# The fourth column block of the last gate's weights as two transfers of 108 and 20 rows

## The chip, the cores and the metric

The kernel runs on one core of a Trainium2 chip. The metric is the device time of one execution in microseconds (us); less is better. Before the change the median of three runs is 242.96 us (242.74 to 242.99).

## What is computed

One decoder step for four rows of batch: a conditioned layer norm, attention over the last 2048 positions of a cache, and a gated feed-forward block. The condition `c` gives six vectors by one matrix; the last of them, `gb`, scales the output of the feed-forward block.

```python
mod = (_silu(c) @ w_mod).reshape(c.shape[0], 6, 1, -1)
sa, ca, ga, sb, cb, gb = (mod[:, 0], ..., mod[:, 5])
h = _layernorm(x) * (1 + ca) + sa
x = x + ga * A(h, k_cache, v_cache, wq, wo)      # 32 heads, 8 groups, 2048 positions, float32
h = _layernorm(x) * (1 + cb) + sb
x = x + gb * ((silu(h @ w1) * (h @ w3)) @ w2)    # 512 -> 1792 -> 512
```

All data is float32. Some 100 MB of caches and weights are read once from HBM, and the four rows of batch need little arithmetic on each byte.

## The kernel before

**Staging.** Two buffers of 128 rows (partitions) by 16384 columns, `KV[0]` and `KV[1]`, take the keys and values of the eight groups in turn; `WP` takes the projection weights. When the last groups are done, the same buffers take the weights of the feed-forward block. `KV[1]` then holds, from left to right: the second part of w3 (columns 0 to 6143, in two transfers on the semaphores `df2a` and `df2b`), the last gate's weights `gb_in` (columns 6144 to 8191, four column blocks of 512, one for each 128 rows of the contraction, on `dgb`), and w2 (14 chunks of 512 columns in six transfers of 4, 4, 2, 2, 1 and 1 chunks, each on a semaphore of its own, `dw[0]` to `dw[5]`).

**Order of the transfers.** All large transfers but one are issued by SyncE (SP) through the helper `load` (L89), in the order in which the code has them; ACT issues the first projection weights and `x_in` (4 rows of 512 columns) at the start (L92, L93). SP waits on semaphores of the compute engines before a buffer is written again. After `o_done` has reached 8 (L120) it issues the two parts of w3, `gb_in` and the six parts of w2 without a further wait; then it waits for `last` and stores the output (L482).

**Order of the work at the end.** TensorE's order is that of the code. After the norm it multiplies by w1 and a part of w3 (`bQ`), by the rest of w3 (`bA`), and transposes the products. Then it waits for `dgb` (L443) and computes the gate in four products, one for each column block (`bM`, L445). ACT copies it to `gb_sb`. Then TensorE goes through w2: it waits for `dw[i]` before part i (L455). The first eight chunks are summed in `bO`, the last six in `bX`, to which `bO` is brought by `y_sb`. After the last part VectorE multiplies by the gate (`yt`, L478), adds the residual (`y`, L480), and SP stores `y`.

A semaphore of a transfer rises by 16 when the whole transfer has landed. `KV<-w_in` in a row of the profile is a transfer or a wait for w2 at this place, since the input names are shown without their digits; `KV<-f_in` is w1 or w3.

Of the kernel before, what the change touches and what calls it, by code (L numbers as in the profile page):

```python
# [43 lines left out]
def block_kernel(nc, x_in, t0_in, t1_in, kv_in, w_in, wm_in, f1_in, f2_in, gb_in, w2_in, out):  # L44
    T, v, s, gp, S = nc.tensor, nc.vector, nc.scalar, nc.gpsimd, nc.sync

    def sems(names):
        return [nc.alloc_semaphore(n) for n in names.split()]

    def sb(name, cols, rows=P):  # L50
        return nc.alloc_sbuf_tensor(name, (rows, cols), F32).ap()
# [8 lines left out]
    dx, dt0, dt1, dkv, dk, dva, dvb, dwo, dm, df1, df2a, df2b, dgb = sems("dx dt0 dt1 dkv dk dva dvb dwo dm df1 df2a df2b dgb")  # L60
# [5 lines left out]
    KV = [sb("KV0", 16384), sb("KV1", 16384)]  # L66
# [21 lines left out]
    def load(dst, src, sem):  # L88
        S.dma_start(dst, src).then_inc(sem, 16)  # L89
# [30 lines left out]
    S.wait_ge(o_done, G)  # L120
    load(KV[1][:, :3072], f2_in[:, :3072], df2a)
    load(KV[1][:, 3072:6144], f2_in[:, 3072:], df2b)
    load(KV[1][:, 6144:8192], gb_in, dgb)
    for a, b, sem in zip(W2_CUTS[:-1], W2_CUTS[1:], dw):
        load(KV[1][:, 8192 + a * 512 : 8192 + b * 512], w2_in[:, a * 512 : b * 512], sem)

# [313 lines left out]
    t_hid = V.op(v.tensor_mul(view(hidT)[:, :, :3], view(sT)[:, :, :3], view(bS)[:, :, :3, :B]))  # L440


    T.wait_ge(dgb, 16)  # L443
    for k in range(4):
        ins = mm(bM[32 * k : 32 * k + B, :], sc[:, k * B : (k + 1) * B], KV[1][:, 6144 + 512 * k : 6144 + 512 * (k + 1)])  # L445
    ins.then_inc(pe, 1)
# [85 lines left out]
```

## Time and profile before

| | us |
|---|---|
| median of three runs | 242.96 |
| the profiled execution | 243.09 |
| its span, first to last instruction | 241.7 |

The profile is that of one execution. Its span is divided by engine: PE is TensorE's matrix multiply, DVE is VectorE, ACT is ScalarE, SPq is the queue of SyncE from which transfers are issued. "DMA share" is the mean busy share of the core's 16 DMA engines; a share of 0.25 says that on average four of the 16 were moving data. It can pass 1 a little where packets overlap at their ends, and in short stretches a packet is counted with the stretch in which it lies, so single steps of 0.1 us are rough. A packet is what one engine moves at a time: a row of a transfer, at most 64 KB, and at the end of a transfer a word of 4 bytes for the semaphore on each engine that took part. The chain that ended last is followed back from the last instruction to what released it.

### The profile page before, as it was taken

The numbers are of one execution on the slowest core, as the hardware profiler recorded it, in microseconds if no ns is written. First come the engines' busy times: TensorE is split into PE (matmuls) and PEld (weight loads), VectorE is DVE, ScalarE is ACT, GpSimd is POOL, SyncE is SP. The second block draws the span as 40 slices with busy tenths as digits, with TensorE's granted clock in tenths as the row PEclk, the third lists the DMA queues.
The fourth block names the chain that finished last, engine by engine and source line by source line (L and its number), as shares of the span: only waits on it lengthen the run. The fifth ranks groups of instructions, "written<-read, shape, count | busy, mean of one in ns | idle before, by whom it ended". The sixth has DMA issues, their size and how long they took to land. (4 is left out here: it accounts for less than half of the span.)

```text
span 241.7 us, 2238 instructions
## 1 busy us (share of the span) xinstructions
PE 137.8 (57%) x940; PEld 38.0 (16%) x940; DVE 38.6 (16%) x126; ACT 25.1 (10%) x54; POOL 1.7 (1%) x14
## 2 busy tenths in 40 slices
PE   3004677726771478267713782877137869656964
PEld 0000122201220013112200130121001312111211
DVE  3003203202200022022000220130002222133112
ACT  2002002100010011010100110011002100133110
POOL 2000000000000000000000000000000000000000
PEclk9999959968798579887985898679758997995999
DMA  7998989899989898999898989998989999999993
GB/s 266 440 511 358 510 361 499 369 423 439 504 369 499 369 499 370 423 428 504 369 499 369 499 369 423 434 510 369 499 347 445 442 396 445 449 431 394 413 415 116
DMA packets 4045, 101.34 MB, mean 419 GB/s; under 512 B 452, under 2 KB 580, under 8 KB 1096
## 3 DMA queue, kind: packets, MB, share of 16 engines
q1 hardware_dynamic: 3888, 99.17, 95.7%
q10 hardware_dynamic: 152, 2.11, 2.1%
q8 instruction: 3, 0.05, 0.1%
q14 instruction: 2, 0.02, 0.0%
HBM read 101.20 MB, written 0.07 MB: 419 GB/s over the span
## 5 line engine op out<-in xcount | busy, mean ns | idle before, releaser
L266 PE MATMUL bS<-KV,Z 128*16 128x512 f32 x256 | 42.7, 828 | 39.2 <-PEq L269 39.2
L266 PE MATMUL bO<-KV,pT 128*16 128x512 f32 x256 | 32.5, 652 | 0.5
L266 PEld LDWEIGHTS bS<-KV,Z 128*16 128x16 f32 x256 | 9.3, 123 | 67.1 <-issue 67.1
L222 DVE TENSOR_REDUCE MX<-bS 128x1 f32<-128x512 f32 x8 | 5.5, 692 | 80.4 <-PE bS L266 80.4
L266 PE MATMUL bM<-KV,sc 128*4 128x512 f32 x24 | 6.9, 801 | 16.6 <-DVE sc L188 16.6
L230 ACT ACTIVATE p_sb<-bS,NB 128x512 f32<-128x512 f32 x8 | 5.5, 687 | 101.2 <-DVE NB L228 101.2
L287 PE MATMUL bP<-ident,p_sb 128*128 128x128 f32 x32 | 5.6, 303 | 16.6 <-PEq L269 16.6
L266 PE MATMUL bA<-WP,oT 128*4 128x512 f32 x64 | 11.1, 773 | 4.3 <-PEq L269 4.3
L266 PEld LDWEIGHTS bO<-KV,pT 128*16 128x16 f32 x256 | 8.2, 107 | 23.9 <-issue 23.9
L251 ACT ACTIVATE o_sb<-bO,LB 128x512 f32<-128x512 f32 x8 | 5.5, 687 | 48.8 <-PE bO L266 48.8
L266 PE MATMUL bQ<-WP,hT 128*4 128x512 f32 x64 | 9.2, 647 | 0.6 <-DVE hT L197 0.6
L287 PE MATMUL bX<-ident,o_sb 128*128 128x128 f32 x32 | 5.0, 280 | 7.2 <-PEq L269 7.2
L254 DVE TENSOR_REDUCE oT<-bX 128x16 f32<-128x64 f32 x8 | 1.8, 224 | 43.6 <-PE bX L287 43.6
L287 PEld LDWEIGHTS bP<-ident,p_sb 128*128 128x128 f32 x32 | 3.6, 148 | 24.0 <-issue 24.0
L287 PE MATMUL bT<-ident,q_sb 128*128 128x128 f32 x32 | 5.5, 298 | 3.2 <-PEq L269 3.2
L201 ACT ACTIVATE q_sb<-bQ 128x512 f32<-128x512 f32 x8 | 4.7, 593 | 13.3 <-PE bQ L266 13.3
L287 PEld LDWEIGHTS bX<-ident,o_sb 128*128 128x128 f32 x32 | 3.4, 141 | 14.3 <-issue 14.3
L235 DVE COPY pT<-bP 128x256 f32<-128x256 f32 x8 | 3.4, 424 | 13.5 <-PE bP L287 13.5
L266 PE MATMUL bQ<-KV,h2T 128*4 128x512 f32 x32 | 5.3, 816 | 0.3 <-DVE h2T L398 0.3
L287 PEld LDWEIGHTS bT<-ident,q_sb 128*128 128x128 f32 x32 | 3.6, 150 | 8.0 <-issue 7.7
L266 PEld LDWEIGHTS bM<-KV,sc 128*4 128x4 f32 x24 | 1.0, 104 | 22.4 <-DVE sc L188 18.2
L266 PE MATMUL bX<-KV,sc 128*4 128x512 f32 x24 | 4.2, 592 | 0.0
(100 smaller groups left out, 65.2 us busy)
## 6 DMA issues: line engine op xcount, KB each, us to landing
WP<-w_in SPq DMA_DIRECT2D x3, 4096.0 KB, 22.0
KV<-kv_in SPq DMA_DIRECT2D x1, 4096.0 KB, 24.3
KV<-f_in SPq DMA_DIRECT2D x1, 4096.0 KB, 28.0
KV<-kv_in SPq DMA_DIRECT2D x1, 3072.0 KB, 31.1
KV<-wm_in SPq DMA_DIRECT2D x1, 3072.0 KB, 18.4
KV<-f_in SPq DMA_DIRECT2D x2, 1536.0 KB, 19.2
KV<-t_in SPq DMA_DIRECT2D x1, 2056.0 KB, 12.2
WP<-t_in ACTq DMA_DIRECT2D x1, 2048.0 KB, 12.4
```

The source lines that it names most:

```text
L201: A.op(s.mul(q_sb, bQ, DH**-0.5), q_ok)
L222: t = V.op(v.reduce_max(MX[:, 0:1], bS, axis=AX.X))
L230: A.op(s.activation(p_sb, bS, AF.Exp, bias=NB[:, 0:1], accum_out=SM[:, 0:1]), p_ok)
L235: v.tensor_copy(pT.rearrange("p (t b c r) -> p c b t r", t=NT, b=B, c=4), bP.rearrange("p (c b i) -> p c b i", c=4, b=B)[:, :, :, :16].rea ...
L251: A.op(s.mul(o_sb, bO, LB[:, 0:1]), o_ok)
L254: V.op(v.tensor_reduce(oT.rearrange("p (r b) -> p r b", r=R), diag, axis=AX.X, op=ALU.add), ot_ok)
L266: return T.matmul(o, lhsT, rhs, start=start, stop=stop, skip_group_check=True)
L287: ins = T.transpose(dst[:, c * P : (c + 1) * P], src[:, c * P : (c + 1) * P], ident)
```

## The change

`gb_in` is loaded by three transfers instead of one. The first has 128 rows and the first three column blocks (1536 columns). The fourth block (512 columns) comes in two transfers, rows 0 to 107 and rows 108 to 127. All three are on `dgb`, and TensorE waits for 48 instead of 16 before the gate's products. The bytes and their places are the same, and so is everything else.

```diff
     load(KV[1][:, 3072:6144], f2_in[:, 3072:], df2b)
-    load(KV[1][:, 6144:8192], gb_in, dgb)
+    load(KV[1][:, 6144:7680], gb_in[:, :1536], dgb)
+    for rows in (slice(0, 108), slice(108, 128)):
+        load(KV[1][rows, 7680:8192], gb_in[rows, 1536:], dgb)
     for a, b, sem in zip(W2_CUTS[:-1], W2_CUTS[1:], dw):
         load(KV[1][:, 8192 + a * 512 : 8192 + b * 512], w2_in[:, a * 512 : b * 512], sem)
@@
-    T.wait_ge(dgb, 16)
+    T.wait_ge(dgb, 48)
```

SP's queue from the first part of the feed-forward weights on, the piece of the difference between the two kernels (rows by columns of each transfer; `f_in` with 8192 columns is w1 with a part of w3, `w_in` is w2):

```order
 L89 DMA KV<-f_in 128x8192
 L89 DMA KV<-f_in 128x3072 x2
-L89 DMA KV<-gb_in 128x2048
+L89 DMA KV<-gb_in 128x1536
+L89 DMA KV<-gb_in 108x512
+L89 DMA KV<-gb_in 20x512
 L89 DMA KV<-w_in 128x2048 x2
 L89 DMA KV<-w_in 128x1024 x2
 L89 DMA KV<-w_in 128x512 x2
```

Two more transfers stand ahead of the six of w2; on the other engines no instruction changes its place.

## Rows read from the trace of the kernel before

**Rows 1.** The page: span, DMA packets, and DMA queues (packets, MB, share of 16 engines).

```profile
span 241.7 us, 2238 instructions
...
DMA packets 4045, 101.34 MB, mean 419 GB/s; under 512 B 452, under 2 KB 580, under 8 KB 1096
...
q10 hardware_dynamic: 152, 2.11, 2.1%
q8 instruction: 3, 0.05, 0.1%
q14 instruction: 2, 0.02, 0.0%
```

**Rows 2.** Stretches: busy of PE, PEld, DVE, ACT, POOL, clock, DMA share, GB/s.

```profile
2.00:40.00 38.00, 16.89 (x74) 3.75 (x74) 6.42 (x20) 3.65 (x8) 0.47 (x6) 0.91 1.01 435
...
80.00:120.00 40.00, 25.60 (x172) 7.20 (x176) 5.96 (x21) 3.42 (x7) 0.00 (x0) 0.82 1.01 434
...
220.00:230.00 10.00, 9.47 (x62) 2.07 (x62) 1.30 (x5) 0.81 (x2) 0.00 (x0) 0.81 1.01 426
```

**Rows 3.** Chain that ended last, by time: start, us, what (its end).

```profile
210.14 28.79 DMA KV<-w_in
238.93 0.04 issue
238.97 0.45 PE bX L266 x8
239.42 0.02 issue
239.44 0.30 DVE yt L478
```

**Rows 4.** Timeline of the end: start, us, engine, what [idle before, releaser].

```profile
207.29 0.43 SPq L89 DMA_DIRECT2D KV<-gb_in  x1
207.77 12.21 SPq L89 DMA_DIRECT2D KV<-w_in  x6
...
231.47 1.04 PE L266 MATMUL bM<-KV,sc 128*4 128x512 f32 x8
...
232.77 1.04 PE L266 MATMUL bO<-KV,hidT 128*4 128x512 f32 x8 [0.26 <-DMA KV<-w_in]
...
235.16 1.04 PE L266 MATMUL bO<-KV,hidT 128*4 128x512 f32 x8 [1.14 <-DMA KV<-w_in]
...
236.44 0.62 PE L266 MATMUL bX<-KV,hidT 128*4 128x128 f32 x16 [0.24 <-DMA KV<-w_in]
...
237.71 1.05 PE L266 MATMUL bX<-KV,hidT 128*4 128x128 f32 x24 [0.29 <-DMA KV<-w_in]
238.36 0.11 PEld L266 LDWEIGHTS bX<-KV,hidT 128*4 128x4 f32 x8 [0.32 <-DMA KV<-w_in]
238.97 0.11 PEld L266 LDWEIGHTS bX<-KV,hidT 128*4 128x4 f32 x8 [0.50 <-DMA KV<-w_in]
```

**Rows 5.** Page, DMA issues: transfer, issuer, count, size, us to landing.

```profile
KV<-gb_in SPq DMA_DIRECT2D x1, 1024.0 KB, 22.8
```

**Rows 6.** Short stretches at the end; the last two figures are DMA share and GB/s.

```profile
236.80:237.00 0.20, 0.20 (x12) 0.00 (x0) 0.17 (x1) 0.00 (x0) 0.00 (x0) 1.00 1.16 379
237.00:237.10 0.10, 0.10 (x8) 0.08 (x8) 0.00 (x0) 0.00 (x0) 0.00 (x0) 1.00 0.44 164
237.10:237.20 0.10, 0.10 (x8) 0.03 (x8) 0.00 (x0) 0.00 (x0) 0.00 (x0) 1.00 0.28 102
...
237.80:237.90 0.10, 0.10 (x8) 0.10 (x9) 0.00 (x0) 0.00 (x0) 0.00 (x0) 1.00 0.17 62
237.90:238.00 0.10, 0.10 (x12) 0.10 (x8) 0.00 (x0) 0.00 (x0) 0.00 (x0) 1.00 0.10 41
...
238.20:238.30 0.10, 0.10 (x8) 0.00 (x0) 0.00 (x0) 0.00 (x0) 0.00 (x0) 1.00 0.11 41
238.30:238.40 0.10, 0.07 (x8) 0.04 (x8) 0.00 (x0) 0.00 (x0) 0.00 (x0) 1.00 0.05 20
...
238.50:238.60 0.10, 0.10 (x8) 0.00 (x0) 0.00 (x0) 0.00 (x0) 0.00 (x0) 1.00 0.01 0
```

**Rows 7.** DMA queues in 33.8 to 34.0 us: packets, MB, share of 16 engines.

```profile
q8 instruction: 1, 0.02, 32.2%
```

**Rows 8.** DMA queues in 14.5 to 14.8 us, where the packets of `x_in` lie.

```profile
q10 hardware_dynamic: 4, 0.01, 7.0%
```

## The prediction

> **What bounds the kernel now.** I read the stretches first. From 2 us on the 16 DMA engines are busy all the time: the share is 1.01 in the first 40 us, in the middle and from 220 to 230 us [rows 2]. No compute engine is near that over the whole span. The chain that ended last says the same of the end: it goes back from the last product over the last transfer of w2, which landed at 238.93 us; behind it come only 0.45 us of TensorE, two VectorE instructions and the store [rows 3]. So what counts is when the last DMA engine has moved its last packet.
>
> The third view is the short stretches at the end [rows 6]. The engines don't stop together. Until 237.0 us all 16 are busy; in 237.0 to 237.1 the share is 0.44, and in the next step it is 0.28, which is 4 to 5 engines. It is 0.17 (three) up to 237.9, 0.10 to 0.11 (two) up to 238.3, then 0.05 (one), and 0.01 from 238.5 on. So 12 engines have done their part by about 237.1 and four are late. I put their ends at about 237.5, 237.85, 238.3 and 238.5 us and call them L1 to L4. The landing that the chain shows (238.93) is L4's end and 0.4 us more. A transfer has landed only when its slowest engine is done, so L4 alone sets the time of the kernel.
>
> Why are they late? All transfers but `x_in` have 128 rows and load the engines alike. Queue q10 has 152 packets [rows 1]: 128 rows and 16 words for the 128-row transfer, which leaves 8, four rows and four words, for `x_in`. What is not alike are the five instruction packets on q8 and q14 [rows 1]: one of q8 took 32.2% of 16 engines for 0.2 us [rows 7], which is 1.03 us of one engine, in the middle of full load. An engine with such a packet stays behind by it to the end, since the queue never runs dry.
>
> **The change part by part.** *What an engine has to do.* Before, each engine moves 8 rows of `gb_in`, 64 KB. In 128-row transfers the time of an engine goes with the size: TensorE's waits for w2 end at 232.77, 235.16, 236.44, 237.71, 238.36 and 238.97 [rows 4], so 1 MB takes 2.4 us, half of it 1.27, and a quarter 0.61 to 0.65 us. Three quarters then take some 1.84 us, so an engine that has no row of the fourth block saves 0.6 us. This is an estimate from these rows.
>
> *Who gets rows of the fourth block.* Both kinds of transfer in the trace share the rows equally: 128 rows are 8 for each of 16 engines, and 4 rows are one for each of four [rows 1]. By equal shares 108 rows go to 12 engines, 9 each, and 20 rows to 10 engines, 2 each. A row of 2 KB costs 0.084 us by `x_in` (7.0% of 16 engines in 0.3 us for four packets [rows 8]) and 0.08 us by the last part of w2 (0.61 to 0.65 us for 8 rows [rows 4]). I take 0.08. If the ten are among the twelve, ten engines get 11 rows, 0.88 us: 0.28 us more than the 0.6 saved, and with two further words 0.3. Two engines get 9 rows, 0.72 us: 0.13 us more. Four get none: 0.6 us less. The sum over the engines is about nil, as it must be: the change only moves work from four engines to twelve.
>
> [...]
>
> *What the end does.* The gain is that of the engine that is last after the change. The 12 early engines go from 237.1 to 237.4 at most, far below 238.5, so 0.3 us on them is hidden by the late ones. If all four late engines are spared, the last is L4 at 237.9: 0.6 us earlier. Each late engine that is not spared moves up by 0.3 us instead. From the rows alone it can't be told which engine is which. I followed the packets in the trace from one to the next on each engine (each starts as the one before it ends). This is no row of a view, so I use it only to choose: the large instruction packets, which made L3 and L4, lie on engines that had no packet of `x_in`; L2's lies on one that had. If the engines of `x_in` are among the ten, as a nested choice would have it, L2 goes from 237.85 to 238.15, and is the new last. Then the end moves from 238.5 to 238.15: 0.35 us earlier.
>
> *Behind the last landing* nothing changes: 0.45 us of TensorE, the two VectorE instructions and the store. The waits for w2 ahead of it move by the same amount. That TensorE is no new bound there I read from the idle times before the parts: 0.26, 1.14, 0.24, 0.29 us and on the weight loads 0.32 and 0.50 [rows 4]; the first product of w2 can't start before the gate's products end at 232.51, and would want to at 232.4, which costs nothing behind it, since it has 1.14 us of idle time before the next.
>
> *The wait for 48.* `gb_in` landed 22.8 us after its issue at 207.29 [rows 4, 5], so at 230.1; the gate's products start at 231.47. They are held by TensorE's own order, with 1.4 us to spare. The last of the three transfers can be 0.3 us later. The wait costs nothing; without that cover it would cost these 0.3 us, and what is queued behind it is the whole of w2.
>
> *Two more issues on SP.* An issue takes 0.43 us there, so w2's first part is issued 0.9 us later, at 208.6 instead of 207.8. Its data is used at 232.77. The six issues of w2 lasted 12.21 us [rows 4], far more than six times 0.43: the queue was full and SP was held until about 220. With two more ahead, the last two or three parts of w2 are issued when a transfer further back has landed, at 224 to 228 us by the transfers' order, an estimate; the data of the last part moves at about 238. The cover is 10 us. Cost nothing.
>
> **The rivals.** *All four spared.* The 12 engines leave out L1 to L4 together: 0.6 us less, 242.4. For it: four late and four spared. Against: the packet on one of `x_in`'s engines, above.
>
> *L4 spared, L3 loaded.* L3 goes to 238.6 (or 238.4 with 9 rows): between 0.1 less and 0.1 more, about 243.0. [...]
>
> *L4 loaded.* The worst engine is among the ten: 0.3 us more, 243.3. Nothing in the rows speaks against it but the packets that I followed, which leave 12 engines for L4, of which four are spared.
>
> *Rows of short transfers disturb each other: slower.* [...] `x_in` with four rows ran at 0.084 us a row [rows 8], which speaks against it, but only 8 KB. If 2 KB took twice as long, the ten engines would have 0.9 us more on top of 0.3. On L4 that gives 244.1, on an engine like L2 239.0, 0.5 more than now: 243.5. It decides from 0.1 us a row on if L4 is loaded. [...]
>
> *The change doesn't do what it says:* the rows are spread over all 16 engines. Then an engine has 8 or 9 rows of 2 KB instead of a quarter of its 8 KB rows: between 0.05 and 0.15 us more on each, 243.05.
>
> **How the numbers follow.** The profiled execution took 243.09, 0.13 above the median of the three runs, which is inside their spread; differences are applied to the median. The chances: L3 and L4 spared, L2 loaded 0.40 (242.96 - 0.35 = 242.6); all spared 0.12 (242.4); L3 loaded or the rows spread over all 0.22 (243.0); L4 loaded 0.18 (243.3); disturbed 0.08 (243.5 to 244.1). The forecast is 242.6. The range leaves out some of the second and all of the last: 242.35 to 243.35. A measurement of this kernel can tell 0.2%, 0.49 us, from no change. Faster by that takes all of L1 to L4 spared, or a little luck with the first: 0.17. Slower takes the last rival, or L4 loaded with a little of it: 0.11. The rest, 0.72, is within.
>
> **What would show it.** In short stretches at the end, the share should fall later for the many (to 237.4 instead of 237.1) and end sooner for the last (238.15 instead of 238.5). The number of packets should rise by 128 for the rows and by 22 words (12 and 10); by 32 words if all 16 engines take part. The landing of the last part of w2 in the chain should be at 238.6 instead of 238.93, and the gate's products should still start at 231.5 with no wait for `gb_in`. If the last landing is at 239.2, L4 was loaded. If 2 KB rows take over 0.1 us, they disturb each other. The forecast is wrong if the late engines of this execution aren't the same in others.

## The result

The change makes the kernel slower: 244.19 us (median of 8 runs, 243.38 to 244.68) against 242.98 us for the kernel before (8 runs, 242.74 to 243.19). The ratio is 1.0044, with a 95% interval of 1.0028 to 1.0061. The forecast was 242.6, with a range up to 243.35, so it was wrong in sign and range. The traced execution took 243.63 us with a span of 242.2; it is one of the shorter ones of the changed kernel.

The page's DMA line of the changed kernel (packets, bytes, mean rate), which answers to the second line of [rows 1]:

```profile
DMA packets 4195, 101.34 MB, mean 418 GB/s; under 512 B 474, under 2 KB 602, under 8 KB 1374
```

There are 150 packets more than before: 128 for the rows, and 22 words. So the packets agree with 108 rows on 12 engines and 20 on 10, as was forecast. By that count the load was uneven as meant.

The end of the chain that ended last (start, us, what), beside [rows 3]:

```profile
219.29 20.18 DMA KV<-w_in
239.47 0.04 issue
239.51 0.45 PE bX L268 x8
239.96 0.02 issue
239.98 0.30 DVE yt L480
```

It is the same chain; its last landing is at 239.47 instead of 238.93 us. Short stretches at the end of the changed kernel (the last two figures are DMA share and GB/s), beside [rows 6]:

```profile
237.60:237.80 0.20, 0.20 (x8) 0.05 (x8) 0.00 (x0) 0.00 (x0) 0.00 (x0) 1.00 0.83 318
237.80:238.00 0.20, 0.14 (x8) 0.00 (x0) 0.00 (x0) 0.00 (x0) 0.00 (x0) 1.00 0.93 358
238.00:238.20 0.20, 0.00 (x0) 0.00 (x0) 0.00 (x0) 0.00 (x0) 0.00 (x0) 1.00 0.42 154
238.20:238.40 0.20, 0.15 (x8) 0.15 (x12) 0.00 (x0) 0.00 (x0) 0.00 (x0) 1.00 0.35 133
...
238.80:239.00 0.20, 0.19 (x10) 0.11 (x8) 0.00 (x0) 0.00 (x0) 0.00 (x0) 1.00 0.11 41
239.00:239.10 0.10, 0.10 (x8) 0.00 (x0) 0.00 (x0) 0.00 (x0) 0.00 (x0) 1.00 0.01 0
```

Two things are to be seen. Most engines are busy until 238.0 instead of 237.0 to 237.1, 0.9 us later, where 0.3 was forecast. And the last stops 1.0 us after the many, where it was 1.4 us before. So the ends did draw together, by 0.4 us, but both moved back: the many by 0.9 us, the last by 0.5.

Where that time went is seen in the stretch in which the gate's weights are moved. First the kernel before, then the changed one, 227 to 231 us (columns as above):

```profile
227.00:231.00 4.00, 2.94 (x23) 0.74 (x17) 1.82 (x5) 0.22 (x1) 0.00 (x0) 1.00 1.01 422
```

```profile
227.00:231.00 4.00, 4.00 (x28) 0.92 (x22) 1.13 (x4) 0.76 (x2) 0.00 (x0) 1.00 1.02 314
```

The engines are just as busy, 1.01 and 1.02, but they move 314 GB/s instead of 422. In 4 us that is 0.43 MB less, which is 1.0 us of all 16 engines at the old rate. So packets take longer. Taken one by one from the two traces, the packets of 8 KB in this stretch lasted 0.41 us on the mean instead of 0.31, and the new ones of 2 KB lasted 0.12 us. This is what has to be explained.

Two other parts of the prediction can be read off at once. The gate's products and SP's queue, beside [rows 4] (timeline of the changed kernel):

```profile
207.96 1.26 SPq L89 DMA_DIRECT2D KV<-gb_in  x3
...
209.26 13.21 SPq L89 DMA_DIRECT2D KV<-w_in  x6
...
232.29 1.04 PE L268 MATMUL bM<-KV,sc 128*4 128x512 f32 x8
```

The products start with no wait for `gb_in` before them; they are 0.8 us later than in [rows 4] because TensorE's own work ahead of them is, and TensorE still waits over 1 us for w2 behind them. SP is done with its issues by 222.5 us (224 to 228 was estimated), 16 us before the last data has moved. Neither the wait for 48 nor the two issues cost anything.

### The profile page after: what moved, and what is told of

Read it like the earlier page. It is cut to its first block, busy times and chain, and to the rows that moved or that the text cites. A ratio compares the mean times of both kernels' runs of the same rounds, so it can differ in the third digit from the quotient of the medians.

```text
span 242.2 us, 2240 instructions
## 1 busy us (share of the span) xinstructions
PE 136.5 (56%) x940; PEld 37.8 (16%) x940; DVE 38.6 (16%) x126; ACT 25.1 (10%) x54; POOL 1.7 (1%) x14
## 5 line engine op out<-in xcount | busy, mean ns | idle before, releaser
L268 PE MATMUL bS<-KV,Z 128*16 128x512 f32 x256 | 43.6, 844 | 42.9 <-PEq L271 42.9
L268 PE MATMUL bM<-KV,sc 128*4 128x512 f32 x24 | 6.1, 724 | 16.5 <-DVE sc L190 16.5
L268 PE MATMUL bA<-WP,oT 128*4 128x512 f32 x64 | 10.2, 715 | 3.0 <-PEq L271 3.0
L268 PE MATMUL bQ<-WP,hT 128*4 128x512 f32 x64 | 8.3, 592 | 0.6 <-DVE hT L199 0.6
L268 PE MATMUL bQ<-KV,h2T 128*4 128x512 f32 x32 | 5.8, 886 | 0.3 <-DVE h2T L400 0.3
```

What stands on the lines that cost most here:

```text
L268: return T.matmul(o, lhsT, rhs, start=start, stop=stop, skip_group_check=True)
```

## The experiments

The theory (C) is a guess: a DMA engine that writes rows which in a full transfer (all 128 rows) belong to another engine collides with that one, and both get slower. No trace names the engine of a packet, so which rows belong to which engine, and whether two engines meet, isn't shown; C's forecasts by row below rest on an assumption about that. The runs show which rows cost time. Its rivals: the two more transfers themselves (Q), the uneven load (U), and short transfers as such (S). Times are medians, with the kernel before on the same chip behind them. "The rate" is what the DMA engines move from 227 to 231 us.

**The changed kernel again.**

> The changed kernel itself, for a second trace and more times. In its first trace packets of 2, 6 and 8 KB got longer between 227 and 231 us, and 314 GB/s were moved there instead of 422. If the rows of the short transfers disturb the other writes (theory C), that stretch is slow again and the time is again 243.4 to 244.7. If the loss was an accident of one execution, the stretch has some 420 GB/s and the time is 243.0 or less.

Measured: 244.22 us (before 243.07), ratio 1.0047 (1.0034 to 1.0059), and 319 GB/s from 227 to 231 us. The loss is no accident.

**As many transfers, all of 128 rows.**

```diff
-    load(KV[1][:, 6144:8192], gb_in, dgb)
+    load(KV[1][:, 6144:7168], gb_in[:, :1024], dgb)
+    load(KV[1][:, 7168:7680], gb_in[:, 1024:1536], dgb)
+    load(KV[1][:, 7680:8192], gb_in[:, 1536:], dgb)
```

> Three transfers for the last gate's weights as in the change, but each of all 128 rows (1024, 512 and 512 columns), so every engine writes its usual rows and all have the same load. Theory C (rows written by other engines than usual collide): no loss, 243.0 to 243.15, the 0.1 us being packets of 4 and 2 KB in place of 8 KB. Theory Q (two more transfers, issues and waits in SP's queue cost the time): as slow as the change, 244.0 to 244.3.

Measured: 243.23 us (before 243.07), ratio 1.0007 (0.9998 to 1.0016). The same stretch:

```profile
227.00:231.00 4.00, 3.93 (x28) 0.91 (x22) 1.14 (x5) 0.69 (x2) 0.00 (x0) 1.00 1.06 421
```

It has short rows, three issues and a wait for 48, and the full rate. Theory Q falls.

**Two halves of 64 rows.**

```diff
-    for rows in (slice(0, 108), slice(108, 128)):
+    for rows in (slice(0, 64), slice(64, 128)):
```

> The fourth block comes in two halves of 64 rows. [...] Theory C: slow, 243.7 to 244.5, and under 380 GB/s between 227 and 231 us. Theory U (the uneven load of 11, 9 and 0 rows costs the time): 243.0 to 243.15.

Measured: 244.72 us (before 243.07), ratio 1.0063 (1.0050 to 1.0076):

```profile
227.00:231.00 4.00, 2.85 (x19) 0.72 (x16) 1.79 (x5) 0.22 (x1) 0.00 (x0) 1.00 1.06 297
```

By equal shares, an estimate, each engine has 4 rows of each half and the load is even, and the rate is as low as in the changed kernel (297 and 314 GB/s): U falls. The time is 0.5 us longer than that of the changed kernel, but not all of it is the transfers'. In this trace the chain doesn't end with a landing but with TensorE's products for w2, which had a granted clock of 0.50 from 235 to 240.6 us; in the changed kernel they have 1.00. The end of the chain, and the stretch at that clock:

```profile
236.88 1.89 PE bO L268 x8
238.77 2.65 PE bX L268 x56
...
235.00:240.60 5.60, 5.53 (x60) 1.67 (x56) 0.69 (x1) 0.27 (x1) 0.00 (x0) 0.50 0.67 260
```

**Which rows.** Three pairs of 64-row transfers of the same size, with rows 32 to 95, 16 to 79 and 0 to 63. These kernels leave out the other rows of the block; the second transfer of a pair goes to columns that nothing reads.

```diff
+    for at in (7680, 15360):
+        load(KV[1][32:96, at : at + 512], gb_in[32:96, 1536:], dgb)
```

> The fourth block comes as rows 32 to 95 only, twice (the second time to unused columns), each a transfer of 64 rows; the gate's weights of the other rows are left out. Load, row size and count of transfers are those of the run with 64 and 64 rows. [...] Theory C (only rows that are another engine's usual rows collide): 243.0 to 243.3, over 400 GB/s from 227 to 231 us. Theory S (short transfers of less than 128 rows are slow whatever their rows): 244.2 to 245.1.

> The same with rows 16 to 79, twice. [...] Theory C: the slowest of the three, 244.7 to 246.5. Theory S: the same as rows 32 to 95.

> The same with rows 0 to 63, twice. [...] Theory C: between the two others, 244.0 to 245.2. Theory S: the same as rows 32 to 95.

Measured: 243.18, 244.80 and 245.15 us (before 243.02), ratios 1.0008 (0.9999 to 1.0017), 1.0069 (1.0055 to 1.0083) and 1.0080 (1.0066 to 1.0094). The stretch in the three kernels, in this order:

```profile
227.00:231.00 4.00, 2.76 (x19) 0.73 (x16) 1.82 (x5) 0.22 (x1) 0.00 (x0) 1.00 1.02 412
```

```profile
227.00:231.00 4.00, 3.89 (x28) 0.91 (x22) 1.18 (x5) 0.66 (x2) 0.00 (x0) 1.00 1.05 266
```

```profile
227.00:231.00 4.00, 2.86 (x19) 0.72 (x16) 1.73 (x5) 0.22 (x1) 0.00 (x0) 1.00 1.06 291
```

This decides against S: only the first row differs, and the rate goes from 412 to 266 GB/s. The rows read from HBM move along with the rows written; the folded kernel below tells them apart, for it reads all 128 rows of the block and writes them to rows 32 to 75 alone, at 414 GB/s. So it is the rows written that count. That rows 32 to 95 are free and the two others are not is what C forecast; which two engines meet, and that engines meet at all, isn't shown. The order of the last two can't be told. Rows 0 to 63 were forecast between the others; their rate (291 GB/s) is, but their median is the longest. The two kernels' runs overlap (244.45 to 245.46 us, and 244.31 to 245.19 with rows 16 to 79), and in the trace with rows 0 to 63 too TensorE had the 0.50 clock at the end, and ends the chain; its mean granted clock of 0.832 is the lowest of that kernel's five executions (0.839 to 0.844 in the others).

**How much.** Half of the columns split, and all four blocks in halves of 64 rows:

```diff
-    load(KV[1][:, 6144:7680], gb_in[:, :1536], dgb)
+    load(KV[1][:, 6144:7936], gb_in[:, :1792], dgb)
     for rows in (slice(0, 108), slice(108, 128)):
-        load(KV[1][rows, 7680:8192], gb_in[rows, 1536:], dgb)
+        load(KV[1][rows, 7936:8192], gb_in[rows, 1792:], dgb)
```

```diff
+    for rows in (slice(0, 64), slice(64, 128)):
+        load(KV[1][rows, 6144:8192], gb_in[rows, :], dgb)
```

> As the change, but only the last 256 columns of the gate's weights go as 108 and 20 rows (128 KB instead of 256). If the loss goes with the bytes that unusual engines write, half of it: 243.5 to 243.8. If it goes with the number of such transfers, 244.1 to 244.4. If 108 and 20 rows of 1 KB gain what was hoped and collide little, 242.8 or less.

> All four blocks of the gate's weights in two halves of 64 rows (8 KB rows, two transfers instead of one): four times the bytes of the run with 64 and 64 rows of the fourth block, without short packets. If the loss goes with these bytes, 246 to 250. If it came from short rows of 2 KB, 243.0 to 243.3.

Measured: 243.85 and 247.81 us (before 243.12), ratios 1.0031 (1.0018 to 1.0043) and 1.0183 (1.0167 to 1.0198). 0.73 us for 128 KB in 108 and 20 rows, 1.2 for 256 KB; 1.65 us for 256 KB in halves, 4.7 for 1 MB. The loss grows with the bytes, less than in proportion, and rows of 8 KB lose too (199 GB/s from 227 to 231 us).

**Alone in the queue.** SP waits before and behind the fourth block, once with 108 and 20 rows, once with 128.

```diff
     load(KV[1][:, 6144:7680], gb_in[:, :1536], dgb)
+    S.wait_ge(dgb, 16)
     for rows in (slice(0, 108), slice(108, 128)):
         load(KV[1][rows, 7680:8192], gb_in[rows, 1536:], dgb)
+    S.wait_ge(dgb, 48)
```

> The change, but SP waits until the 1536-column transfer has landed before it issues the two short ones, and until these have landed before w2. The two then run with nothing else in the queue; the gaps cost some us, so only the packets count. If the short rows collide with the other streams (writers of their usual rows), 2 KB takes 0.084 us as elsewhere, and 12 engines need some 0.9 us for both. If they collide among themselves, 2 KB takes 0.1 us or more on the mean.

> The pair to the run before it: the same waits in SP's queue, but the fourth block in one transfer of 128 rows. 2 KB takes 0.084 us under either theory.

With the waits the one execution of each took 248.10 and 248.29 us, so only the packets are compared. Packets of the block (queue, packets, MB, share of 16 engines), the first from 230.3 to 232.7 us, the second from 230.5 to 232.7:

```profile
q1 hardware_dynamic: 150, 0.26, 43.0%
```

```profile
q1 hardware_dynamic: 144, 0.26, 36.7%
```

43.0% of 16 engines for 2.4 us is 16.5 us, 36.7% for 2.2 us is 12.9 us. So the mean over 128 rows is 0.13 and 0.10 us. Even 128 rows alone are above 0.084, so the figure that was to decide doesn't. One by one, the median row takes 0.084 us in both; a minority of longer rows, up to 0.71 and 0.34 us, lifts the means, and they aren't explained. The difference, 3.6 us of engine time, is small beside what is lost in the queue (1.0 us of 16 engines). Most of the loss seems to come from meeting other transfers; this is a hint, not a proof.

**At the very end.** The gate's weights as before, the last transfer of w2 split.

```diff
+    for rows in (slice(0, 108), slice(108, 128)):
+        load(KV[1][rows, 8192 + 13 * 512 : 8192 + 14 * 512], w2_in[rows, 13 * 512 :], dw[5])
```

> The gate's weights as before; instead the very last transfer of w2 (512 columns) is split into 108 and 20 rows. The unevenness that was meant to help comes where the 12 early engines have nothing else to do. Theory C: the collisions hit little but these rows; L3 and L4 save 0.6 us, L2 gets 0.24 us more (11 rows instead of 8), and the time is 242.6 to 243.0. Theory X (the split rows are bad by themselves, wherever they stand): 243.5 or more.

Measured: 243.74 us (before 243.07), ratio 1.0028 (1.0018 to 1.0039). This missed what theory C had been made to say: the loss is there too. First the kernel before, then this one:

```profile
236.00:237.00 1.00, 0.76 (x20) 0.32 (x16) 0.69 (x1) 0.00 (x0) 0.00 (x0) 1.00 1.04 379
```

```profile
236.00:237.00 1.00, 0.75 (x20) 0.32 (x16) 0.63 (x1) 0.00 (x0) 0.00 (x0) 1.00 1.07 322
```

The engines still move the parts of w2 ahead of the split one, and these get later: TensorE's wait for the fourth part ends at 238.32 us instead of 237.71 [rows 4], and in this trace (243.17 us) that wait is the last; the two parts behind it have landed when TensorE comes to them.

**Are the late engines among the spared?** Rows 32 to 83, and 32 to 75, in place of 32 to 95, twice as there; the other rows of the block are left out. By equal shares 52 rows are 4 for each of 13 engines and 44 rows 4 for each of 11, so three and five engines are spared; the packets counted in the last section agree.

```diff
-        load(KV[1][32:96, at : at + 512], gb_in[32:96, 1536:], dgb)
+        load(KV[1][32:84, at : at + 512], gb_in[32:84, 1536:], dgb)
```

> [...] If L3 and L4 are among the three, 242.4 to 242.7 (0.4 to 0.7 less than 243.18, and L2 is the new last). If only L4 is, 242.9 to 243.0. If L4 is not, 243.1 to 243.3.

> [...] If the second of the two latest engines is one of the two that are now spared besides, 242.4 to 242.7. If it is among the 11 that have rows, so that the change loads it, 242.9 to 243.2 as with rows 32 to 83.

Measured: 243.03 (before 243.05) and 242.61 us (before 243.07), ratios 0.9997 (0.9988 to 1.0006) and 0.9986 (0.9977 to 0.9995). Short stretches at the end, first with rows 32 to 95, then with rows 32 to 83, then with rows 32 to 75:

```profile
238.10:238.30 0.20, 0.20 (x16) 0.08 (x4) 0.00 (x0) 0.00 (x0) 0.00 (x0) 1.00 0.13 51
238.30:238.50 0.20, 0.20 (x12) 0.04 (x8) 0.00 (x0) 0.00 (x0) 0.00 (x0) 1.00 0.13 51
238.50:238.70 0.20, 0.20 (x8) 0.07 (x8) 0.00 (x0) 0.00 (x0) 0.00 (x0) 1.00 0.06 21
```

```profile
238.10:238.30 0.20, 0.20 (x12) 0.07 (x8) 0.00 (x0) 0.00 (x0) 0.00 (x0) 1.00 0.05 20
238.30:238.50 0.20, 0.20 (x8) 0.04 (x8) 0.00 (x0) 0.00 (x0) 0.00 (x0) 1.00 0.03 10
```

```profile
237.70:237.90 0.20, 0.20 (x12) 0.02 (x3) 0.00 (x0) 0.00 (x0) 0.00 (x0) 1.00 0.08 31
237.90:238.10 0.20, 0.20 (x9) 0.10 (x8) 0.00 (x0) 0.00 (x0) 0.00 (x0) 1.00 0.06 20
238.10:238.30 0.20, 0.20 (x8) 0.01 (x3) 0.00 (x0) 0.00 (x0) 0.00 (x0) 1.00 0.00 0
```

With all 16 engines loaded two of them (0.13) are busy until 238.5. With three spared it is one or less (0.05, 0.03), and with five spared both are done by 238.1. So by these traces, one of each, 13 loaded engines spare one of the two latest and 11 spare both. Of the times only that of 11 is clear of the kernel before; 243.03 isn't clear of it, nor of 243.18. The change loads 12. If the engines spared among 13 are spared among 12 too, as a nested choice would have it, one of the two latest is spared, and the other is either spared too or has 9 rows. Which of these wasn't told apart.

**The idea without the loss of rate, complete.** The 128 rows of the fourth block are laid three times side by side over rows 32 to 75 (44, 44 and 40 rows), with the condition laid out to match and zero in the other rows, and the gate's fourth product becomes a sum of three; once for 512 columns, once for 256.

```diff
+FOLD = [(0, 44), (44, 44), (88, 40)]
+FAT = [7680, 15360, 15872]
+    for (a, n), at in zip(FOLD, FAT):
+        load(KV[1][32 : 32 + n, at : at + 512], gb_in[a : a + n, 1536:], dgb)
...
+    for j, at in enumerate(FAT):
+        ins = mm(bM[96 : 96 + B, 0:], sc[:, 16 + B * j : 16 + B * (j + 1)], KV[1][:, at : at + 512], j == 0, j == 2)
```

> [...] Eleven engines get 12 rows of 2 KB (the eleventh 8), five get none. The two latest save 0.6 us, L2 gets 0.3 us more: 242.5 to 242.8. If L2 or the two more transfers and products eat it up, 242.9 to 243.2; if collisions come back, 243.5 or more.

> The same with the last 256 columns of the block only: half of the shift. The two latest save 0.3 us and stay the last: 242.7 to 242.95.

Measured: 243.19 (242.65 to 243.69) and 242.99 us (before 243.05), ratios 1.0004 (0.9995 to 1.0013) and 0.9998 (0.9989 to 1.0007). The loss of rate is gone (414 GB/s from 227 to 231 us in the first), and the median is no gain. In the trace of the first, an execution of 242.65 us, the DMA engines are done early, but TensorE no longer has slack:

```profile
237.00:237.50 0.50, 0.22 (x9) 0.00 (x0) 0.50 (x1) 0.00 (x0) 0.00 (x0) 1.00 0.54 205
237.50:238.00 0.50, 0.40 (x16) 0.39 (x20) 0.04 (x1) 0.00 (x0) 0.00 (x0) 1.00 0.20 78
238.00:238.70 0.70, 0.70 (x29) 0.43 (x24) 0.00 (x0) 0.00 (x0) 0.00 (x0) 1.00 0.01 3
```

From 238.0 us on next to nothing is moved, and PE is busy all of the time. That isn't so in every execution. In the one traced later (242.81 us) the chain ends with a landing again, at 238.74 us:

```profile
219.38 19.36 DMA KV<-w_in
238.74 0.04 issue
```

Both traced executions are shorter than the kernel before (243.05), so neither says why the median is half a us above the first.

**Longer executions.**

> The changed kernel once more, for a trace of one of its longer executions (244.1 to 244.7). If the collisions of the split rows vary, the packets between 227 and 231 us are longer still. If the late engines differ, the last landing lies further behind the others and that stretch is as before.

> The same, a second chance for a longer execution, with the same two outcomes.

> The folded kernel (no colliding rows, uneven load) once more, whose runs spread from 242.65 to 243.69. A trace of a longer execution shows whether the same engines are late: if its last landing is later with no long packets, it is the late engines, not collisions, that vary.

Measured, one execution each: 243.46, 243.56 and 242.81 us, again from the short end, with 332, 326 and 412 GB/s in the stretch. The question stays open.

## Why the prediction was wrong

*The bound, the shares, the covers.* The bound is right: the end is the last landing of w2, before and after. The equal shares agree with the count (150 packets more), and neither the wait for 48 nor SP's issues cost anything. The other signs went the wrong way: the many stop at 238.0 us and not at 237.4, the last at 239.0 and not at 238.15, and the last landing is at 239.47 and not at 238.6. A row of 2 KB took 0.12 us, and over 0.1 was the prediction's own sign of rows that disturb each other.

*The late engines.* The likeliest case had L3 and L4 spared. By the traces with 13 and 11 loaded engines, one of the two latest is; the other is spared or has 9 rows. Without the loss of rate the uneven load is worth about what the sum said: 243.18 with 16 engines loaded, 242.61 with 11, which is 0.57 us for the 0.6 that a spared engine saves. That kernel leaves out part of the block, though, and adds nothing to L2.

*The step that failed* is "Who gets rows of the fourth block", where a row of 2 KB was costed at 0.08 us wherever it goes, and a spared engine at a clean 0.6 us less. Both prices hold in the runs that start at row 32: 0.085 us for a row of 2 KB with rows 32 to 95, and the 0.57 us above. When the rows are split at 108, packets get longer, also those of 6 and 8 KB that the change doesn't split. From 227 to 231 us, one by one: 2 KB takes 0.121 us (0.085 with rows 32 to 95), 6 KB 0.288 (0.238), 8 KB 0.412 (0.314 before). Over the 128, 42 and 90 rows of that stretch this is about 5, 2 and 9 us of engine time, 1.0 us of all 16 engines. That is more than the whole gain, and most of it lies on rows that the prediction left at their old price. The last engine was to end 0.35 us earlier and ended 0.5 later.

*The rival was there, but mis-sized in chance and in kind.* "Rows of short transfers disturb each other" had 0.08 and reached 243.5 to 244.1, which is near the 244.19 measured. It was held down by `x_in`: 0.084 us a row [rows 8]. It was the nearest row, and it showed no loss. But `x_in` is 8 KB in all, and the least that was split here is 128 KB; why its four packets were spared isn't shown. In what way rows disturb each other isn't shown either; the runs show longer packets, 0.121 us for 2 KB and 0.412 for 8 KB. And the rival priced only the split rows, not the streams they hit. What the runs show is 412 against 266 GB/s for the same two transfers of 64 rows, by the first row alone.

*Spread.* The changed kernel's runs spread over 1.3 us, those of the kernel before over 0.45. The loss of rate isn't the whole of it: the folded kernel keeps its rate (414 GB/s) and spreads over 1.0 us, and the kernels with 13 and 11 loaded engines, no slower than the kernel before (243.03 and 242.61), over 0.9 and 1.0, while rows 32 to 95 (412 GB/s), by equal shares with the same load on all, spread over 0.3. The traces of the changed kernel are all of shorter executions, so the 0.6 us between the traced 243.63 and the median 244.19 isn't accounted for.

## What to carry to other kernels

Splitting a transfer by rows can slow other transfers in flight as well. It did so here for 108 and 20 rows (314 GB/s from 227 to 231 us, 422 before) and for 64-row transfers from rows 0 and 16 (291 and 266), and not for those from row 32 (412). Why those from row 32 are free isn't shown. When a change moves work from a late engine to early ones, ask which rows the early ones will write and whether a trace shows the price of just those, and give a kind of transfer that the trace doesn't show a range that reaches from a gain to a clear loss. And read GB/s beside the DMA share: here a share of 1.02 at 314 GB/s meant longer packets, not more data.

## What the runs showed of the hardware that was not expected

The same 256 KB in two 64-row transfers cost 0.16 us more than the kernel before, or 1.8 to 2.1 us, by the first row alone (243.18, 244.80 and 245.15, before 243.02); in the trace of the last TensorE's lower clock (0.50) has a part in it. The packets of the transfers of 52 and 44 rows agree with 13 and 11 engines: the pages count 4175 and 4155 packets, 130 and 110 more than before, which is twice 52 rows and 13 words, or twice 44 and 11. And the lateness of single engines at the end was worth 0.57 us (243.18 and 242.61) when five engines, by the traces the two latest among them, had nothing of the block to move.
